# A new instruction order for a gated recurrence with a GEGLU block: weight gates out, crossbar transposes and some of the loads and stores on ScalarE's queue

## Chip, cores and metric

One core of a Trainium2 chip. The metric is the device time of one execution in microseconds (us). Each kernel was executed several times; "fast runs" are the executions that are not over 1.5% above the fastest one of the same kernel, and comparisons use these. The profile of a kernel is one of its executions; its span is some 2 us shorter than the device time. In profile lines PE is TensorE (PEld its weight loads), DVE VectorE, ACT ScalarE, POOL GpSimd and SP SyncE; a q behind a name stands for that engine's instruction queue. PSUM is the memory to which TensorE writes its results; "on-chip memory" in this text is SBUF, where the other tiles lie.

## The reference

A recurrence over 768 positions, for 4 batches of 8 heads of 48 channels, followed by a GEGLU block over 3072 tokens:

```python
mag = np.sqrt(a_re * a_re + a_im * a_im)
scale = np.minimum(mag, 0.999) / (mag + 1e-06)
a_re_n, a_im_n = (a_re * scale, a_im * scale)
for t in range(S):                       # S = 768
    new_re = ar * S_re - ai * S_im       # ar, ai: a_re_n, a_im_n at t
    new_im = ar * S_im + ai * S_re
    S_re, S_im = (new_re + kv, new_im)   # kv = outer product of k and v at t
    y[:, :, t] = np.einsum('bhd,bhde->bhe', q[:, :, t], S_re)
# x = y as (3072, 384)
g = x @ w_gate                           # 384 -> 1536
gelu = 0.5 * g * (1.0 + erf(g * inv_sqrt2))
return gelu * (x @ w_val) @ w_out        # 1536 -> 384
```

## The kernel before

The sequence is cut into 24 chunks of 128 positions. A chunk's decays are cumulated as logarithms (magnitude) and phases, `q` and `k` are multiplied by them and "rotated" into `pair` (cosine and sine parts), and attention within the chunk plus a carried state gives `x`; then come the three products of the GEGLU block. The order is no scheduler's: a text lists about 1240 words, one per step, and the kernel emits them in that order, each engine running its own in order. A word is a step, its chunk, the engine (V VectorE, A ScalarE, P GpSimd, S a crossbar transpose by DMA, B a phase shift that reads PSUM) and the buffer slot:

```python
PLAN = """
ldaim2=0 si2V=0 ldare1=0 tab.LE la1=0 r1 ldare0 la0 r0 ldaim1 si1V ldare2 sr1A la2 sr0A ad1P sr2V ldaim0 r2 ln1=0
# ... (the rest cut) ...
"""
def load(nm, c, slot):                     # q, k, v, a_re, a_im
    # ... (cut) ...
    nc.sync.dma_start(out=t, in_=src[b, :, n * L:(n + 1) * L, :].transpose([1, 0, 2]))

def load_weight(piece, after):
    # ... (cut) ...
    if after:                              # the gate: a small cast that waits for another load
        # ... (cut) ...
        nc.gpsimd.tensor_copy(out=t[:, 0, 0:1], in_=a)
    nc.gpsimd.dma_start(out=t, in_=src)

def pb(c, slot, eng):                      # phase shift of a quarter turn
    t = take("ph", ("ph", c), slot).rearrange("p s h d -> p s (h d)")
    if eng == "B":                         # from PSUM
        nc.vector.tensor_scalar(out=t[:, 0], in0=T["cumt", c], scalar1=TURN / (2.0 * PI),
                                scalar2=TURN / 4.0, op0=ALU.mult, op1=ALU.add)
    else:                                  # from on-chip memory: "ph<-ph" in the profile
        nc.vector.tensor_scalar(out=t[:, 0], in0=t[:, 1], scalar1=TURN / 4.0, scalar2=None, op0=ALU.add)

def rotate(t, i, e, cs, eng):              # kp and qp: "pair<-ke,cs" and "pair<-qe,cs"
    ENG[eng].tensor_tensor(out=t[:, :, i, :, 0:D], in0=e.unsqueeze(2).to_broadcast([128, H, 2, D]),
                           in1=cs.rearrange("p s h d -> p h s d"), op=ALU.mult)

def tps(c, hg, slot, eng):
    t = take("tps", ("tps", c, hg), slot)
    if eng == "S":                         # a crossbar transpose instead of TensorE and a copy
        src = T["pair", c][:, hg * 4:(hg + 1) * 4].rearrange("p h i s d -> p (h i s d)")
        nc.sync.dma_start_transpose(out=t, in_=src)
    else:
        copy(eng, t, T["tp", c, hg])
```

## Time and profile before

| | before |
|---|---|
| median of 3 runs | 252.74 us (252.19 to 254.98) |
| the profiled run, a further one: time, span, TensorE clock granted | 255.99 us, 254.2 us, 0.972 |
| VectorE, ScalarE, GpSimd busy | 181.3, 197.4, 117.5 us |
| crossbar transposes, all issued by SyncE | 30 of `pair`, 17 of `x` |
| ScalarE's table loads | 43 |

TensorE is the fullest engine (82% of the span; ScalarE has 78%) and works to the end, so what counts is where TensorE stands still. The prediction shows the main lines of this profile. Two stretches more, in the columns of the prediction's table of stretches:

```profile
54.00:84.00 30.00, 27.40 (x402) 24.42 (x400) 27.59 (x48) 27.68 (x39) 23.73 (x29) 1.00 1.08 189
84.00:112.00 28.00, 25.28 (x248) 19.38 (x247) 21.62 (x39) 22.52 (x36) 15.63 (x15) 0.94 0.77 155
```

And the durations of VectorE's operations by line (ns, least/median/greatest):

```profile
L350 DVE TENSOR_SCALAR ph<-ph x12: 346/352/2336, 20.5 to 219.3; 128x384 int32<-128x384 int32 x12
L368 DVE TENSOR_TENSOR pair<-ke,cs x11: 541/549/559, 24.7 to 197.1; 128x768 bf16<-128x768 bf16 x11
L274 DVE TENSOR_TENSOR z<-aim,z x12: 545/550/1018, 8.6 to 162.9; 128x384 f32<-128x384 f32 x12
```

In this profile most operations of one shape share one duration, 352 ns for the phase shift; yet three of the twelve took 1159, 1743 and 2336 ns.

### The profile page before, as it was taken

To read this page: it belongs to the slowest core of one execution; us is meant where nothing else is said; L and a number is where in the kernel's file an instruction comes from. 1 tells how busy PE (TensorE), PEld (TensorE's weight loads), DVE (VectorE), ACT (ScalarE), POOL (GpSimd) and SP (SyncE) were. 2 spreads that over 40 slices of the span, in tenths; PEclk is the share of its full clock that TensorE was granted. 3 is DMA by queue.
4 is the path that set the end of the run, shared out by engine and by line. 5 is a ranking of instruction groups with operands and counts; after the bars stand their busy time and mean duration, and the time that the engine had idled before them with its cause. 6 is when DMAs were issued, how large, how long until landed. Compare 5 with 4: busy or idle time off the path is not lost.

```text
span 254.2 us, 5703 instructions
## 1 busy us (share of the span) xinstructions
PE 207.5 (82%) x2203; PEld 162.4 (64%) x2203; DVE 181.3 (71%) x321; ACT 197.4 (78%) x298; POOL 117.5 (46%) x128
## 2 busy tenths in 40 slices
PE   0125985397999999699798986999699999998994
PEld 0002654377987777487586675787686868887782
DVE  4648998298989699499597576986786556827350
ACT  4998999288899999576989788799699868735141
POOL 3211392698995783222577536623490722150000
PEclk9999997589999999799999999999999999999999
DMA  7989999999999196999999999989976696175121
GB/s 145 242 199 203 197 211 181 172 218 211 152 188 226 22 207 137 208 173 192 221 189 172 195 219 172 196 159 192 198 143 133 118 162 167 33 158 56 49 93 62
DMA packets 166059, 41.75 MB, mean 164 GB/s; under 512 B 157841, under 2 KB 165265, under 8 KB 166033
## 3 DMA queue, kind: packets, MB, share of 16 engines
q1 hardware_dynamic: 162848, 37.86, 75.5%
q0 software_dynamic: 3184, 3.54, 8.5%
q8 instruction: 17, 0.28, 0.5%
q14 instruction: 10, 0.07, 0.1%
HBM read 30.67 MB, written 4.72 MB: 139 GB/s over the span
## 4 chain that ended last, share of the span: by engine, by line
PE 36%; DMA 19%; DVE 12%; ACT 12%; issue 9%; SPq 7%; POOL 2%; POOLq 1%; DVEq 0%; ACTq 0%
PE bank L447 18%; PE bank L469 12%; SPq L230 6%; DMA k<-in_k_dram 5%; ACT L483 4%; DMA tps<-pair 4%; DMA wg<-in_moe_w_gate_dram 4%; DMA are<-in_a_re_dram 3%; DMA xt<-x 3%; DVE h L461 2%; ACT gel L457 2%; PE bank L398 2%; PE bank L323 2%; ACT cs L354 2%; DVE ssb L401 1%
## 5 line engine op out<-in xcount | busy, mean ns | idle before, releaser
L447 PE MATMUL bank<-xt,wg 128*128 128x256 bf16 (+1 forms) x468 | 56.7, 268 | 6.8 <-DMA xt<-x 5.0
L457 ACT ACTIVATE gel<-bank 128x512 bf16<-128x512 f32 x72 | 39.8, 599 | 27.1 <-PE bank L447 20.1
L461 DVE TENSOR_TENSOR h<-bank,gel 128x512 bf16<-128x512 f32 x72 | 47.4, 684 | 16.4 <-PE bank L447 11.0
L483 ACT ACT_TABLE_LOAD x43 | 55.2, 1283 | 1.5 <-PEq L509 0.8
L447 PE MATMUL bank<-xt,wv 128*128 128x256 bf16 (+1 forms) x468 | 55.2, 264 | 0.3 <-ACT gel L457 0.2
L469 PE MATMUL bank<-wo,h 128*128 128x384 bf16 x288 | 49.6, 326 | 1.6 <-ACT e L334 1.4
L447 PEld LDWEIGHTS <-wg 128*128 128x128 bf16 x468 | 42.1, 99 | 13.5 <-issue 4.0
L447 PEld LDWEIGHTS <-wv 128*128 128x128 bf16 x468 | 41.8, 98 | 5.8 <-issue 0.6
L401 DVE TENSOR_TENSOR ssb<-bank,tri 128x512 bf16<-128x512 f32 x48 | 32.3, 683 | 16.8 <-PE bank L398 13.3
L469 PEld LDWEIGHTS <-h 128*128 128x128 bf16 x288 | 27.5, 98 | 18.8 <-issue 1.9
L368 POOL TENSOR_TENSOR pair<-ke,cs 128x768 bf16<-128x768 bf16 x13 | 21.9, 1682 | 15.3 <-PE bank L469 6.7
L291 POOL TENSOR_TENSOR are<-are,s 128x384 f32<-128x384 f32 x16 | 16.4, 1030 | 21.7 <-DVE s L280 11.6
L368 POOL TENSOR_TENSOR pair<-qe,cs 128x768 bf16<-128x768 bf16 x9 | 15.5, 1724 | 18.9 <-issue 11.0
L398 PE MATMUL bank<-tps 128*128 128x128 bf16 x192 | 18.4, 223 | 5.8 <-DMA tps<-pair 2.4
L398 PEld LDWEIGHTS <-tps 128*128 128x128 bf16 x192 | 13.5, 100 | 10.1 <-issue 2.9
L354 ACT ACTIVATE cs<-ph 128x768 bf16<-128x768 int16 x24 | 19.4, 836 | 0.6 <-DVE ph L341 0.5
L333 ACT ACTIVATE e<-bank 128x384 bf16<-128x384 f32 x24 | 11.8, 491 | 6.5 <-PE bank L323 6.4
L362 POOL TENSOR_TENSOR qe<-q,e 128x384 bf16<-128x384 f32 x13 | 12.0, 925 | 10.2 <-ACT e L334 8.1
L382 PE MATMUL bank<-ident,pair 128*128 128x128 bf16 x144 | 12.4, 244 | 4.5 <-POOL pair L368 4.0
L211 DVE COPY tps<-bank 128x1024 bf16<-128x1024 bf16 x18 | 12.0, 681 | 5.6 <-PE bank L382 5.6
L274 POOL TENSOR_TENSOR z<-aim,z 128x384 f32<-128x384 f32 x12 | 12.9, 1084 | 4.8 <-ACT z L263 4.7
L359 POOL TENSOR_TENSOR ke<-k,e 128x384 bf16<-128x384 f32 x12 | 12.1, 1006 | 5.4 <-ACT gel L457 3.7
(79 smaller groups left out, 337.0 us busy)
## 6 DMA issues: line engine op xcount, KB each, us to landing
v<-in_v_dram SPq DMA_DIRECT2D x24, 192.0 KB, 4.1
q<-in_q_dram SPq DMA_DIRECT2D x24, 192.0 KB, 3.9
k<-in_k_dram SPq DMA_DIRECT2D x24, 192.0 KB, 3.8
out_dram<-o SPq DMA_DIRECT2D x24, 192.0 KB, 2.3
aim<-in_a_im_dram SPq DMA_DIRECT2D x21, 192.0 KB, 3.8
are<-in_a_re_dram SPq DMA_DIRECT2D x21, 192.0 KB, 3.8
wo<-in_moe_w_out_dram POOLq DMA_DIRECT2D x3, 384.0 KB, 6.2
wg<-in_moe_w_gate_dram POOLq DMA_DIRECT2D x1, 768.0 KB, 9.6
```

The lines of the kernel that those rows point to most:

```text
L230: nc.sync.dma_start(out=t, in_=src[b, :, n * L:(n + 1) * L, :].transpose([1, 0, 2]))
L274: ENG[eng].tensor_tensor(out=t, in0=block("aim", c), in1=t, op=ALU.mult)
L291: ENG[eng].tensor_tensor(out=t, in0=t, in1=block("s2", c), op=ALU.add)
L354: act(out=take("cs", ("cs", c), slot).rearrange("p s h d -> p (s h d)"), in_=lo[:, :, 0], func=AF.Sin, scale=2.0 * PI / TURN)
L368: ENG[eng].tensor_tensor(out=t[:, :, i, :, 0:D], in0=e.unsqueeze(2).to_broadcast([128, H, 2, D]), in1=cs.rearrange("p s h d -> p h s d"), ...
L398: nc.tensor.matmul(ps[:, hi, :], t[:, 2 * hi + 1, :], t[:, 2 * hi, :], start=True, stop=True)
L401: nc.vector.tensor_tensor(out=take("ssb", ("ssb", c, hg), slot), in0=T["sc", c, hg], in1=tri.unsqueeze(1).to_broadcast([128, 4, 128]), op= ...
L447: nc.tensor.matmul(ps[:, a], w[:, i, fc * 128:(fc + 1) * 128], T["xt", c][:, 0:n, i, :], start=(i == 0), stop=(i == NDM - 1))
L457: act(out=take("gel", ("gel", c, f), slot), in_=T["g", c, f], func=AF.Gelu)
L461: nc.vector.tensor_tensor(out=t[:, f * FW * L:(f + 1) * FW * L], in0=T["v", c, f], in1=T["gel", c, f], op=ALU.mult)
L469: nc.tensor.matmul(ps, ht[:, fc, i, :], wo_sb[:, fc, :], start=(fc == 0), stop=(fc == NFF - 1))
L483: nc.scalar.preload_act_table_set(TABLES[word[4:]])
```

## The change

The intent: SyncE's queue, which issued everything but the weights, is full in the middle of the kernel. All crossbar transposes move to ScalarE's queue, with 20 of 116 loads and 11 of 24 stores; the gates of the weight loads go; a search found a new order for two queues. In the new order ScalarE has 34 table loads instead of 43 and fewer casts and squares; VectorE has more (17 `kp` rotations instead of 11, 30 phases read from PSUM instead of 23), GpSimd 7 `kp` instead of 13, and TensorE transposes ten more sets itself (22 of `pair` instead of 18, 13 of `x` instead of 7).

```diff
-def load(nm, c, slot):
+crossbar = nc.scalar.dma_start_transpose
+def load(nm, c, slot, eng):
+    queue = nc.scalar if eng == "A" else nc.sync
-    nc.sync.dma_start(out=t, in_=src[...])
+    queue.dma_start(out=t, in_=src[...])
-    if after:
-        # ... (cut) ...
-        nc.gpsimd.tensor_copy(out=t[:, 0, 0:1], in_=a)
-    nc.sync.dma_start(out=out[c * L:(c + 1) * L, :], in_=T["o", c])
+    (nc.scalar if eng == "A" else nc.sync).dma_start(out=out[c * L:(c + 1) * L, :], in_=T["o", c])
-    if eng == "S":                       # tps and xt
-        nc.sync.dma_start_transpose(out=t, in_=src)
+    if eng == "D":
+        crossbar(out=t, in_=src)
-ldaim2=0 si2V=0 ldare1=0 tab.LE la1=0 r1 ldare0 la0 r0 ldaim1 si1V ldare2 sr1A la2 sr0A ad1P ...
+ldare2A=0 tab.LE la2=0 r2 ldare0 sr2V ldare1 ldaim1=0 ldaim0 ldaim2 la0 sr0P r0 la1 ldare3=1 ...
 (all other lines of the order differ as well)
```

## The prediction

> **What bounds the kernel now.** I read the page from its top: the busy shares, the 40 slices, then the waits of the issuing queue, then the chain that ended last, and then a table of stretches.
>
> ```profile
> PE 207.5 (82%) x2203; PEld 162.4 (64%) x2203; DVE 181.3 (71%) x321; ACT 197.4 (78%) x298; POOL 117.5 (46%) x128
> ...
> PE   0125985397999999699798986999699999998994
> ...
> ACT  4998999288899999576989788799699868735141
> ...
> DMA  7989999999999196999999999989976696175121
> ```
>
> No engine is full over the whole span, but PE is nearly full after its first eight or nine slices, and the DMA engines are nearly full for most of the first 28. The table of stretches (columns: length, then busy us and instructions of PE, PEld, DVE, ACT and POOL, PE clock, DMA share, GB/s) shows it in stages:
>
> ```profile
> 0.00:54.00 54.00, 25.84 (x229) 17.35 (x230) 37.72 (x78) 43.04 (x69) 23.62 (x36) 0.91 0.98 196
> ...
> 112.00:140.00 28.00, 25.16 (x276) 19.55 (x275) 23.38 (x40) 25.16 (x41) 15.36 (x14) 1.00 1.03 189
> 140.00:180.00 40.00, 34.48 (x338) 26.25 (x336) 30.52 (x53) 34.25 (x48) 19.20 (x18) 1.00 0.95 191
> 180.00:225.00 45.00, 44.60 (x481) 35.91 (x482) 29.44 (x51) 34.98 (x51) 18.95 (x19) 1.00 0.69 134
> ```
>
> The first 54 us are a fill: PE idles 28 us of them while loads arrive. From 54 us on PE is busy 181.7 of 200 us, so of the whole span at most 28 + 18 = 46 us of PE idleness can be attacked, and some 11 us at the start (the wait for the first phase angles, "ACT th" 11.4 us) can hardly be. In the middle PE, ACT and DMA all stand near 0.9 together: a balanced pipeline in which a queue that comes late is felt.
>
> That queue is SyncE's. It issues everything except weights, in order. Its own waits and the issue durations of its two transposes (ns, min/median/max) say:
>
> ```profile
> SPq L436 <- DVE x L211: 10.2, 2, 7.8
> ...
> SPq L388 <- POOL pair L368: 8.5, 3, 6.2
> ```
> ```profile
> L388 SPq DMA_TRANSPOSE tps<-pair x30: 1231/1352/3165, 87.3 to 227.4; - x30
> ```
>
> A transpose holds the queue 1.35 us and, while its input is late, it holds all loads and stores behind it too. With about 0.6 us a load and 0.56 us a store (read off the SyncE timeline after 100 us) the queue issues 116 x 0.6 + 24 x 0.56 + 30 x 1.35 + 17 x 1.21 = 144 us; between 87 and 190 us its timeline is issue after issue with hardly a gap. The chain that ended last carries the same signature:
>
> ```profile
> PE 36%; DMA 19%; DVE 12%; ACT 12%; issue 9%; SPq 7%; POOL 2%; POOLq 1%; DVEq 0%; ACTq 0%
> PE bank L447 18%; PE bank L469 12%; SPq L230 6%; DMA k<-in_k_dram 5%; ACT L483 4%; DMA tps<-pair 4%; DMA wg<-in_moe_w_gate_dram 4%; DMA are<-in_a_re_dram 3%; DMA xt<-x 3%; DVE h L461 2%; ACT gel L457 2%; PE bank L398 2%; PE bank L323 2%; ACT cs L354 2%; DVE ssb L401 1%
> ```
>
> The two crossbar transposes are 7% (some 17 us) of the chain, load issue 6%, the first gate weight 4%.
>
> **What the Trainium skill says.** (1) "DMA: Bandwidth & Descriptors", section "Issuing engines are not separate DMA queues": all issuers share the same 16 DMA engines, and a second issuer only saves sequencer time. The trace agrees in part: in the first 54 us the DMA share is 0.98 at 196 GB/s, so there a second queue can't bring bandwidth; but from 87 to 190 us the sequencer itself is full, so its time is worth saving. (2) The same page, "Silent corruption: two transposing streams in flight at once": transposes from SyncE and ScalarE must not overlap, which is why all of them move together; no run here shows the corruption. (3) "Perfetto Trace Analysis", sections "DVE / Act Engine Instruction" and "DMA Instruction — HWDGE": a compute instruction waits in a queue of its own while the sequencer goes on, whereas a DMA instruction keeps the sequencer through its wait, the lock on the descriptor generator and the generation. So on ScalarE a DMA issue may hide under activations that were already queued, but a late input stops everything behind it. ScalarE issues nothing in this trace, so how much hides is open; the growth of the same transpose from 1.23 to 3.17 us agrees with waits on a shared resource. (4) "ScalarE: Activation LUTs", "What ACT_TABLE_LOAD costs": about 1283 ns a load, and the trace has exactly 1283 ns; the extra drain of 1380 ns that the page adds isn't seen (the next activation starts about 1.29 us after the load starts).
>
> **The change part by part.**
>
> *ScalarE, compute.* Counting the words of the two orders: table loads 43 to 34, -9 x 1.283 = -11.5 us; phases -9 x 0.50 = -4.5; squares -8 x 0.52 = -4.2; casts of x -4 x 0.48 = -1.9; casts of v -3 x 0.51 = -1.5; one xt copy -0.5; st +2 x 0.48 = +1.0; five new evictions of 128x1024, estimated at 1.05 us from 0.48 us for 384 and 0.84 us for 768 columns, +5.3. Sum -17.8: 197.4 becomes about 180 us.
>
> *ScalarE, issue.* New: 26 tps x 1.35 = 35 us, 11 xt x 1.21 = 13, 20 loads x 0.6 = 12, 11 stores x 0.56 = 6: 66 us. If nothing hid, ScalarE would have 246 us of work, against a span of 254 whose last 29 us hold only 9.8 us of it: ScalarE would be the bound. I assume that about half hides under queued activations, so 213 us, 16 more than now.
>
> *SyncE.* 96 x 0.6 + 13 x 0.56 = 65 us in place of 144: no longer full, and loads no longer stand behind a transpose whose input is late.
>
> *VectorE.* kp +6 x 0.55, qp +0.7, phases +9 x 0.55, x +4 x 0.55, xt +7 x 0.35, the rest about -2.5: +11 us, to 192. *GpSimd*: six of the 1.68 us kp leave, squares and casts come: -4. *TensorE*: +4 tps and +6 xt sets of transposes, 32 x 86 ns + 18 x 120 ns = +4.9 us. *DMA*: 4 of 30 and 6 of 17 crossbar transposes fewer. *Weight gates*: seven small casts of 0.2 to 0.35 us, about 2 us of GpSimd; the first waits 6.1 us for a k load. PE waits only 1.4 us for that weight, so this is worth 1 to 3 us at the fill; without it the weights compete with the loads.
>
> *By stage* (adding the mean durations, less their overlaps, in program order; estimates). Until ten of 24 outputs are done, at 144 us before: TensorE 117 to 124, VectorE 114 to 128, ScalarE 115 to 116 plus 19 of issue. The fill can therefore hardly be shorter, and VectorE would need 89% instead of 79% to keep 144 us. After it: TensorE 116 to 114, VectorE 71 to 68, ScalarE 76 to 58 plus 45 of issue; before took 110 us here, so ScalarE fits only if the issue hides in part. If the freed queue takes about half of the PE waits on transposes (5.0 + 2.7 + 2.9 + 2.4 = 13 us), most of the 4 us of "ACT gel" waiting for h, and some of the late loads, 9 to 12 us come back; the extra TensorE work costs 5 and ScalarE's issue 2. Net -3 to -5 us: 249 us.
>
> **Rivals.** *A: ScalarE becomes the bound.* For it: 180 + 66 = 246 us and the in-order stop at a late pair (pair waits of 6.2 us stood on SyncE, where they cost only loads; on ScalarE they delay gelu, and so the PSUM banks). Against it: the order was searched anew, moves 18 us off ScalarE, and drops table loads. It would make 256 to 265 us. *B: the freed queue pays in full.* Loads come as soon as buffers are free, transposes no longer queue behind loads, and PE idleness after 54 us falls from 18 to 8 us, the fill by 3: 239 to 244 us. *C: it is all hidden by the DMA engines*, whose share is 0.95 to 1.09 in three of the middle stretches; then only ten transposes fewer count, against 5 us more on TensorE: 250 to 254 us.
>
> **Range and chances.** The arithmetic alone says no change or slightly slower (A and C); that the new order was found by a search, with ScalarE relieved for the purpose, speaks for B. I give B 0.42, C and the middle 0.36, A 0.22. Predicted 249 us, range 239 to 262.
>
> **What would show it.** Right: SyncE's timeline between 87 and 190 us has gaps and its wait for x and pair is gone; ACT busy near 180 us with 34 table loads; xt and tps waits of PE below 7 us; PE busy about 212 us; the first gate matmul near 54 us as before. The share of issue that hides shows as ScalarE's gaps at transposes: half of 66 us would leave some 33 us of them. Wrong: ScalarE idle ahead of gelu with "issue" or its own queue as the cause, and PE waiting for gelu (rival A); DMA share still at 1.0 with the same GB/s and PE waiting for loads (rival C); or a fill that is shorter by over 5 us, which I don't expect since VectorE and the loads bound it.

## The result, and the profile after

| | before | after |
|---|---|---|
| median, runs of the same session | 253.84 us (252.19 to 254.98, 4 runs) | 263.36 us (262.31 to 265.38, 4 runs) |
| ratio of fast runs | 1 | 1.039 (95%: 1.029 to 1.049) |
| profiled span, granted clock | 254.2 us, 0.972 | 261.0 us, 0.961 |

A ratio is the mean time of one kernel's fast runs over the mean of the other's fast runs in the same rounds, so it is not quite the ratio of the medians quoted beside it. The changed kernel is slower by 3.9%.

The page after, the lines that answer to the prediction's first:

```profile
PE 210.4 (81%) x2253; PEld 166.7 (64%) x2253; DVE 198.3 (76%) x343; ACT 182.6 (70%) x271; POOL 119.3 (46%) x127
...
PE   0138566609999999979879999499859999999994
...
ACT  4999995728899899979688896856537367414231
...
DMA  8999999899997009499975999969975947633102
```

ScalarE fell by 14.8 us, about as foreseen (182.6 against 180), and TensorE is at 210.4 (212 foreseen). VectorE rose by 17.0 us, to 198.3; 192 was foreseen. TensorE stops in the ninth slice, and the DMA engines stand still near 90 us. The stretches:

```profile
0.00:54.00 54.00, 25.72 (x244) 17.55 (x244) 46.60 (x87) 44.73 (x67) 28.42 (x37) 0.91 1.12 203
54.00:84.00 30.00, 25.01 (x372) 23.36 (x373) 27.53 (x48) 22.83 (x31) 22.21 (x25) 0.89 1.04 176
84.00:112.00 28.00, 27.96 (x276) 21.63 (x273) 21.19 (x40) 26.52 (x36) 9.96 (x11) 1.00 0.38 66
```

From 84 to 112 us the DMA share is 0.38 and TensorE is busy 27.96 of 28 us: that hole costs nothing there. Over the whole span TensorE has 210.4 - 207.5 = 2.9 us more work and 50.6 - 46.7 = 3.9 us more idleness, together the 6.8 us by which the span is longer. (The profiled run of the kernel before was slower than its four runs in the table, so the two profiles show 7.1 of the 9.5 us between the medians.) Part of the 2.9 us is probably the lower clock, 0.961 against 0.972: between d1 and d2 below, both at 0.986, TensorE's busy time differs by 0.8 us only. That is an estimate; why the clock is lower was not tested. So neither issue time nor DMA bandwidth is visibly the limit. Where is TensorE's idleness? Its longest wait after the fill, and then VectorE's and GpSimd's timelines just before that wait ends (start, duration, engine, line, operation, count; in brackets the idle time before it and what ended it):

```profile
58.84 0.50 PE L428 MATMUL bank<-ident,x 128*128 128x128 bf16 x3 [7.61 <-DVE x L212]
```
```profile
51.35 4.11 DVE L366 TENSOR_TENSOR pair<-ke,cs 128x768 bf16<-128x768 bf16 x1 [2.39 <-POOL ke L357]
55.38 2.94 DVE L348 TENSOR_SCALAR ph<-ph 128x384 int32<-128x384 int32 x3
58.24 0.54 DVE L212 CAST x<-bank 128x384 bf16<-128x384 f32 x1
```
```profile
47.74 0.50 POOL L212 CAST vb<-v 128x384 bf16<-128x384 f32 x1 [9.84 <-DMA v<-in_v_dram]
...
50.40 0.92 POOL L357 TENSOR_TENSOR ke<-k,e 128x384 bf16<-128x384 f32 x1
51.26 0.80 POOL L245 DMA_DIRECT2D wg<-in_moe_w_gate_dram  x1
52.08 1.96 POOL L272 TENSOR_TENSOR z<-aim,z 128x384 f32<-128x384 f32 x2
53.99 0.99 POOL L289 TENSOR_TENSOR are<-are,s 128x384 f32<-128x384 f32 x1
54.94 1.20 POOL L278 TENSOR_TENSOR s<-aim 128x384 f32<-128x384 f32 x1
```

TensorE stands still for 7.61 us until VectorE has copied `x` out of PSUM. VectorE comes to that copy late: it waits 2.39 us for GpSimd's `ke`, then one rotation takes 4.11 us (0.55 is normal) and three phase shifts 2.94 us together (0.35 each is normal). While these run, GpSimd, which had waited 9.84 us for a load of `v`, works without a gap. The copy of `x`, which reads PSUM, takes its normal 0.54 us.

Yet this stop alone doesn't explain the longer time. By 112 us TensorE has been busy 78.7 us here and 78.5 us before (sums of the stretches shown), so until then it stood still as long in both, 33.3 and 33.5 us. The added idleness comes later: 149.0 - 131.7 = 17.3 us against 142.2 - 129.0 = 13.2 us. The largest wait in that part is for crossbar transposes (7.1 us, 2.4 us before). The runs e3 and a2 below each take one of these two waits away.

VectorE's held operations are not only at that place. The same lines as before, over the whole kernel:

```profile
L348 DVE TENSOR_SCALAR ph<-ph x14: 344/704/1801, 55.4 to 207.4; 128x384 int32<-128x384 int32 x14
L366 DVE TENSOR_TENSOR pair<-ke,cs x17: 542/552/4108, 20.8 to 218.4; 128x768 bf16<-128x768 bf16 x17
L272 DVE TENSOR_TENSOR z<-aim,z x13: 546/621/1989, 8.0 to 166.9; 128x384 f32<-128x384 f32 x13
```

The median phase shift has doubled. The Trainium skill, "SBUF — State Buffer", section "Who interferes with whom", has a mechanism for this: VectorE and GpSimd share a pair of ports to on-chip memory. A VectorE instruction with two inputs there contends with a GpSimd instruction that reads; one in the two-port mode (which a `tensor_scalar` can enter) contends with GpSimd too. Whichever comes first keeps the ports for its whole instruction, and the other is shut out. That gives the theory to test.

What of ScalarE's issuing? The issue durations on its queue, and the piece of its timeline where a table load, two transposes and two gelus meet:

```profile
L386 ACTq DMA_TRANSPOSE tps<-pair x26: 1246/1298/2073, 107.7 to 233.4; - x26
```
```profile
140.45 1.28 ACT L481 ACT_TABLE_LOAD   x1
141.12 1.31 ACTq L386 DMA_TRANSPOSE tps<-pair  x1
141.75 1.32 ACT L455 ACTIVATE gel<-bank 128x512 bf16<-128x512 f32 x2
142.66 1.38 ACTq L386 DMA_TRANSPOSE tps<-pair  x1
```

The transposes are issued beside table loads and activations, not between them. And SyncE is not full any more; its largest waits (total us, times, longest) are now stores waiting for outputs:

```profile
SPq L248 <- DVE o L212: 61.8, 6, 17.5
SPq L248 <- DMA q<-in_q_dram: 18.2, 1, 18.2
```

### The profile page after: what moved, and what is told of

It reads as the page before. It is cut to its first block, busy times and chain, and to the rows that moved or that the text cites.

```text
span 261.0 us, 5749 instructions
## 1 busy us (share of the span) xinstructions
PE 210.4 (81%) x2253; PEld 166.7 (64%) x2253; DVE 198.3 (76%) x343; ACT 182.6 (70%) x271; POOL 119.3 (46%) x127
## 4 chain that ended last, share of the span: by engine, by line
PE 41%; DMA 17%; DVE 17%; ACT 8%; SPq 5%; issue 4%; ACTq 2%; POOL 2%; DVEq 0%; POOLq 0%
PE bank L445 23%; PE bank L467 10%; DMA v<-in_v_dram 8%; DMA tps<-pair 6%; SPq L233 5%; DVE pair L366 3%; DVE h L459 2%; PE bank L396 2%; DVE ph L348 2%; DVE ssb L399 2%; PE bank L408 2%; DMA out_dram<-o 2%; DMA are<-in_a_re_dram 2%; PE bank L321 2%; DVE z L272 1%
## 5 line engine op out<-in xcount | busy, mean ns | idle before, releaser
L445 PE MATMUL bank<-xt,wv 128*128 128x256 bf16 (+1 forms) x468 | 57.9, 267 | 0.2
L459 DVE TENSOR_TENSOR h<-bank,gel 128x512 bf16<-128x512 f32 x72 | 48.0, 685 | 12.9 <-PE bank L445 7.8
L445 PEld LDWEIGHTS <-wg 128*128 128x128 bf16 x468 | 42.8, 99 | 5.7 <-DMA xt<-x 0.4
L289 POOL TENSOR_TENSOR are<-are,s 128x384 f32<-128x384 f32 x16 | 17.2, 1078 | 29.5 <-DVE s L278 15.9
L396 PE MATMUL bank<-tps 128*128 128x128 bf16 x192 | 19.0, 229 | 13.2 <-DMA tps<-pair 7.1
L366 POOL TENSOR_TENSOR pair<-qe,cs 128x768 bf16<-128x768 bf16 x8 | 13.4, 1669 | 24.7 <-ACT cs L352 14.5
L396 PEld LDWEIGHTS <-tps 128*128 128x128 bf16 x192 | 13.7, 102 | 16.2 <-DMA tps<-pair 7.8
L360 POOL TENSOR_TENSOR qe<-q,e 128x384 bf16<-128x384 f32 x15 | 14.9, 992 | 8.0 <-ACT e L332 6.5
L212 POOL CAST vb<-v 128x384 bf16<-128x384 f32 x20 | 11.4, 587 | 13.4 <-DMA v<-in_v_dram 13.4
L366 DVE TENSOR_TENSOR pair<-ke,cs 128x768 bf16<-128x768 bf16 x17 | 14.9, 879 | 2.5 <-POOL ke L357 2.4
L380 PE MATMUL bank<-ident,pair 128*128 128x128 bf16 x176 | 14.9, 238 | 1.5 <-DVE pair L366 1.3
L278 POOL TENSOR_TENSOR are<-are 128x384 f32<-128x384 f32 x11 | 9.9, 903 | 12.0 <-ACT z L257 11.9
```

What stands on the lines that cost most here:

```text
L289: ENG[eng].tensor_tensor(out=t, in0=t, in1=block("s2", c), op=ALU.add)
L360: ENG[eng].tensor_tensor(out=take("qe", ("qe", c), slot), in0=T["q", c], in1=T["e", c][:, 0], op=ALU.mult)
L380: nc.tensor.transpose(ps[:, 2 * hi + i, :], T["pair", c][:, hg * 4 + hi, i], ident)
L396: nc.tensor.matmul(ps[:, hi, :], t[:, 2 * hi + 1, :], t[:, 2 * hi, :], start=True, stop=True)
L445: nc.tensor.matmul(ps[:, a], w[:, i, fc * 128:(fc + 1) * 128], T["xt", c][:, 0:n, i, :], start=(i == 0), stop=(i == NDM - 1))
L459: nc.vector.tensor_tensor(out=t[:, f * FW * L:(f + 1) * FW * L], in0=T["v", c, f], in1=T["gel", c, f], op=ALU.mult)
```

## The experiments

Theory G: the loss comes from GpSimd's work standing where VectorE's is, because VectorE is held off (G1) or because GpSimd's own results come late (G2). Rivals: Q, the issuing on ScalarE (or what is issued there) costs; W, the ungated weights do; T, the extra transposes on TensorE do. All ratios are to the kernel before, in the same rounds.

### 1. The new order with other issuers (Q)

```diff
 a1: crossbar = nc.sync.dma_start_transpose;  queue = nc.sync;  stores nc.sync
 a2: crossbar = nc.sync.dma_start_transpose   (loads and stores as in the change)
 a3: queue = nc.sync                          (transposes and stores as in the change)
```

> The changed kernel with every transpose, load and store issued by SyncE again: only the order (and the missing gates) is new. Theory S (issuing on ScalarE costs the time, by holding gelu and evictions behind transposes): back to 248 to 255 us. Theory O (the order itself: ten more sets of TensorE transposes, 17 us more VectorE, weights without gates): stays at 261 us or above. Ratio to before under S 0.98 to 1.01, under O 1.03 or more.

> The changed kernel with the 37 crossbar transposes on SyncE, loads and stores split as in the change. Theory S (the transposes on ScalarE are the costly part, 37 of 68 issues and about 48 of 62 us): 250 to 256 us. Theory O: within 1% of the changed kernel, 261 to 266 us.

> The changed kernel with all loads and stores on SyncE and only the transposes on ScalarE. Theory S: 260 to 266 us, as the transposes stay. A rival L (what hurts is the split of loads and stores: a load on ScalarE goes out only when ScalarE comes to it, and a store on SyncE that waits for its input holds the loads behind it): the ScalarE half of L would give 254 to 259 us here; under the SyncE half of L it stays at 263 or gets worse, since eleven more stores join SyncE's queue.

Measured: a1 265.35 us, 1.041 (1.030 to 1.051; its profiled execution was an outlier of 546 us and isn't used); a2 263.59 us, 1.036 (1.028 to 1.045); a3 262.15 us, 1.027 (1.017 to 1.037). With everything back on SyncE the new order is as slow as with ScalarE. So the issuer isn't the cause: rival Q falls, and so does the hope that the freed queue pays: in this order it is worth nothing that these runs resolve. In a2 TensorE's wait of 7.1 us for crossbar `tps` is gone, and the kernel is no faster.

### 2. Parts of the change in the old order, and stores and weights in the new

```diff
 b1: nc.sync.dma_start_transpose -> nc.scalar.dma_start_transpose   (old order)
 c1: (nc.scalar if eng == "A" else nc.sync).dma_start -> nc.scalar.dma_start   (new order, all stores)
 c2: words ldw2, ldw3 moved behind vb3P and vb4P                     (new order)
 b2: ldw0@k0 -> ldw0, and so for the other six                       (old order, no gates)
 b3: stores nc.sync.dma_start -> nc.scalar.dma_start                 (old order)
```

> The kernel before with only the issuer of its 47 crossbar transposes changed to ScalarE, order and gates untouched. Theory S: slower by 3 to 8%, 260 to 273 us, since ScalarE gets about 60 us of issue on top of 197 us of compute. Theory O: within 1.5% of before, 250 to 256 us.

> The changed kernel with all 24 stores issued by ScalarE (13 of them stood on SyncE). In the changed kernel's trace SyncE waits 61.8 us in six stores for VectorE's copy of o, 17.5 us at the longest, and the DMA engines move 0 to 18 GB/s in two slices around 85 to 98 us meanwhile. Theory P (a store in SyncE's in-order queue keeps the loads behind it back, so the loads arrive late and TensorE starves after 112 us): 254 to 259 us, and the hole in the DMA row is gone. If P is only a side effect: within 1% of the changed kernel, 261 to 266 us.

> The changed kernel with its first two weight loads moved later in GpSimd's order, each behind the cast of a v block that it kept waiting (v took 14 us to land when both weights, 1.5 MB, were issued just before it). Theory G (the ungated weights take the DMA engines from the loads that the fill needs): 256 to 260 us, and the v load lands in 5 us. Rival: the first gate matmul then waits for its weight instead and nothing is won, 261 to 267 us.

> The kernel before without its seven weight gates and nothing else. Theory G: slower by 1 to 3%, 256 to 262 us. Rival (the gates are free, since GpSimd's own order already holds the weights back): within 1%, 251 to 256 us. The prediction's step (gates worth 1 to 3 us of gain) would give 251 to 253 us.

> The kernel before with its 24 stores issued by ScalarE; loads and all transposes stay on SyncE. If relief of SyncE's queue was worth having (13 us of store waits and 13 us of store issue leave it) and short issues hide under queued activations: 247 to 252 us. If ScalarE pays for every issue: 254 to 262 us.

Measured: b1 282.01 us (276.33 to 288.28, so scattered that no fast set could be formed; even its fastest run is 8.7% above the 254.14 us of before in that session). c1 275.0 us, 1.069 (1.062 to 1.077). c2 264.64 us, 1.025 (1.014 to 1.037). b2 256.34 us, 0.993 (0.984 to 1.003). b3 255.56 us, 0.993 (0.984 to 1.001).

Moving the transposes to ScalarE in an order not made for it costs heavily (b1), and so do more stores there in the new order (c1). Removing the gates is harmless in the old order (b2), so the gates aren't the cause by themselves; loading two weights later in the new order (c2) gives back some 1.4 points, not separable from nothing. In c2 GpSimd's wait for `v` is gone from its largest waits, and yet the rotation still takes 3.43 us, the three shifts 3.02 us, and TensorE waits 6.3 us for `x`. So rival W explains a part at best, and the late `v` is not what makes VectorE's operations long.

### 3. Fewer transposes on TensorE (T)

```diff
-tp9.1=3 tps9.1V=3  tp10.1=4 tps10.1V=4  tp11.0=6 tps11.0V=2  tp13.0=2 tps13.0V=0
+tps9.1D=3          tps10.1D=4           tps11.0D=2           tps13.0D=0
-xtp8=0 xt8V=0  xtp9=0 xt9V  xtp11=0 xt11V  xtp13=6 xt13V
+xt8D=0         xt9D         xt11D          xt13D
```

> The changed kernel with eight of its 35 TensorE transpose sets (four of pairs, four of x, blocks 8 to 13) made crossbar transposes on ScalarE instead; TensorE has 4 x 0.69 + 4 x 0.36 = 4 us less to do and VectorE 4 us. Rival W (TensorE's added work is paid one for one, since TensorE is 80% busy and full after 84 us): 258 to 261 us. Theory S (transposes on ScalarE cost more than they save): 264 us or more.

Measured: 275.12 us, 1.067 (1.061 to 1.073). Returning eight sets to the crossbar makes it worse: TensorE now waits for the transposes.

```profile
PE bank L395 <- DMA tps<-pair: 13.3, 2, 9.3
...
PE bank L444 <- DMA xt<-x: 6.7, 3, 2.6
```

Against 7.1 us for `tps` in the changed kernel. The order had its places chosen for TensorE's transposes, so this run can't say what they cost by themselves; it gives rival T no support, and section 5 leaves them in place.

### 4. Phase shifts read from PSUM instead of on-chip memory (G1, a part)

If the `ph<-ph` shifts are what is held off, giving them PSUM as input should help; they keep their work otherwise.

```diff
 e1 (new order): pb6V pb7V pb8V removed; pb6B pb7B pb8B put right behind pa6A, pa7V, pa8V
 e2 (new order): the same for all 14 shifts
 b4 (old order): the same for all 12 shifts
 e3 (new order): e1, and kp4V moved behind the copy xt0V (after x0V)
```

> The changed kernel with three of its 14 phase shifts, those of blocks 6, 7 and 8, computed on VectorE straight from PSUM behind the step that reads the same bank, where the changed kernel computes them later from SBUF to SBUF. Theory D (VectorE is held off by GpSimd's back-to-back SBUF operations: the SBUF-to-SBUF shifts of 0.35 us took 2.9 us together, and 7.8 us in the run with all loads on SyncE, and the key rotation before them 4.1 us, so that x and TensorE's transposes of x came 7 us late at 51 to 58 us): 257 to 260 us, TensorE's wait for x under 3 us. Rival W (it is the ten extra sets of TensorE transposes and the places of the steps): within 1%, 261 to 265 us.

> The changed kernel with all 14 SBUF-to-SBUF phase shifts taken from PSUM instead (each 0.55 us in place of 0.35 us undisturbed, 0.74 us as measured). Theory D: at least as good as with three, 255 to 260 us; VectorE's busy time falls by 2 to 4 us. Rival W: 261 to 266 us.

> The same edit on the kernel before (12 shifts, mean 0.70 us against 0.35 us at best, so some 4 us lost to GpSimd in all, none of it in a place where TensorE waited long). Theory D: 250 to 254 us, 0 to 1.5% faster than before. Rival: no effect or slower by up to 1%.

> e1 with one word more moved: block 4's key rotation, which took 4.1 us on VectorE at 53 us instead of 0.55 us while GpSimd ran back to back, is placed behind the copies that TensorE waits for. Theory D at this place: TensorE's wait of 4.5 us for x goes, the first 84 us hold 3 us less idle time, and the end comes 2 to 4 us earlier than e1 (ratio to before 1.015 to 1.025). If the time saved there is given back later: ratio 1.03 to 1.04 as before.

Measured: e1 265.28 us, 1.032 (1.027 to 1.036); e2 268.54 us, 1.044 (1.038 to 1.049); b4 261.31 us, 1.018 (1.013 to 1.022); e3 262.1 us, 1.027 (1.018 to 1.035). None repairs it; e1, e2 and b4 miss what theory D foretold, and e3 comes near it. In e1 the three shifts are short again, but the rotation behind them is held instead, and TensorE still waits 5.1 us for `x`:

```profile
53.23 4.06 DVE L365 TENSOR_TENSOR pair<-ke,cs 128x768 bf16<-128x768 bf16 x1
```

In e3 that rotation stands behind `x` and a copy that follows it. It is short again, and TensorE's waits for `x` fall to 1.0 us, from 8.1 us in the changed kernel:

```profile
54.03 0.96 DVE L365 TENSOR_TENSOR pair<-ke,cs 128x768 bf16<-128x768 bf16 x1
```
```profile
PE bank L427 <- DVE x L211: 1.0, 2, 0.5
```

So the long stop is gone, and still the kernel is 2.7% slower than before, against 3.9% with the stop and 3.2% in e1; the intervals of the three overlap. The stop is a part of the loss at most. In b4 and e2 the shifts also come at an earlier place in VectorE's order, before other work (they must follow `pa` while the bank still holds the phases), and that may be what costs: b4 loses 1.8%, with VectorE as busy as before (182.3 us), in an order where little was held off. So these runs neither prove nor refute G1; they show that curing one place isn't enough.

### 5. GpSimd almost idle (G against all rivals)

Each of GpSimd's elementwise operations works on its first column only, in both orders. Their outputs are wrong, which doesn't matter for the times. Memory is filled with zeros first, and the exponents are damped so that nothing overflows. All other engines keep every instruction. (In d1 to d4 the zero fills add 8.4 us to GpSimd and 2.8 us to VectorE at the start.)

```diff
+class Narrow:
+    def _n(self, x):
+        return x[(slice(None),) + tuple(slice(0, 1) for _ in x.shape[1:])]
+    def tensor_tensor(self, out, in0, in1, op):
+        nc.gpsimd.tensor_tensor(out=self._n(out), in0=self._n(in0), in1=self._n(in1), op=op)
+    # tensor_copy likewise
+ENG["P"] = Narrow()        # d1: new order, d2: old order
```

> Wrong result on purpose: the changed kernel with each elementwise GpSimd operation on the first of its columns only (and the decay exponents made near zero, so that all numbers stay finite), so that GpSimd is almost idle and cannot hold VectorE off; every instruction and wait stays. Compare with d2, the same in the old order. Theory D (the new order loses more to VectorE waiting on GpSimd, 23 us over the shortest times of the same operations in place of 13, and to GpSimd's own lateness): both become faster, this one by 8 us or more beyond the other, so that d1 over d2 is within 1.5%. Rival W (TensorE work and the places of loads and stores): d1 stays 3 to 5% above d2.

> Wrong result on purpose: the kernel before with the same edit as d1, the control. 240 to 252 us; VectorE's busy time falls by about 10 us, from the waits on GpSimd that go.

Measured: d1 (new order) 251.26 us, 0.982 (0.976 to 0.989); d2 (old order) 252.39 us, 0.990 (0.983 to 0.996). The new order's deficit of 3.9% is gone: d1 over d2 is 0.982 / 0.990 = 0.993. Both have their own queues, gates and transposes unchanged, so none of Q, W and T is needed to explain it. From the pages of d1 and of d2, and from d1 the operations that were held:

```profile
PE 205.3 (83%) x2253; PEld 162.8 (66%) x2253; DVE 178.5 (72%) x347; ACT 182.2 (73%) x271; POOL 42.1 (17%) x148
PE 204.5 (82%) x2203; PEld 160.3 (64%) x2203; DVE 171.9 (69%) x325; ACT 197.1 (79%) x298; POOL 36.6 (15%) x149
```
```profile
49.17 0.56 DVE L382 TENSOR_TENSOR pair<-ke,cs 128x768 bf16<-128x768 bf16 x1 [1.89 <-POOL ke L205]
49.65 0.92 DVE L364 TENSOR_SCALAR ph<-ph 128x384 int32<-128x384 int32 x3
50.49 0.54 DVE L228 CAST x<-bank 128x384 bf16<-128x384 f32 x1
```

The five operations that stretched from 51.35 to 58.78 us in the changed kernel, 7.4 us, take 1.9 us here, `x` is copied at 50.5 instead of 58.2 us, and the wait of 7.61 us isn't among TensorE's waits any more.

VectorE's busy time now has two parts that can be told apart. With GpSimd nearly idle the two orders differ by 178.5 - 171.9 (d2) = 6.6 us: that is VectorE's added work. With GpSimd at work they differ by 198.3 - 181.3 = 17.0 us. The other 10.4 us are stretching; the expectation for d1 has the same difference from another sum, 23 us over the shortest durations in place of 13.

### 6. GpSimd busy, but hardly reading (G1 against G2)

d1 takes away GpSimd's traffic and its lateness at once. Here GpSimd stays about as busy: its first column, then a write of constants into a buffer that nobody reads, as long as the shortest such operation took (for casts next to nothing), then its second column, for which readers wait. Results are wrong again.

```diff
 class Narrow:
     def tensor_tensor(self, out, in0, in1, op):
-        nc.gpsimd.tensor_tensor(out=self._n(out), in0=self._n(in0), in1=self._n(in1), op=op)
+        nc.gpsimd.tensor_tensor(out=self._n(out, 0), in0=self._n(in0, 0), in1=self._n(in1, 0), op=op)
+        nc.gpsimd.memset(busy[:, 0:n], 0.0)      # n by kind: 395 to 1400 columns, casts 1
+        nc.gpsimd.tensor_tensor(out=self._n(out, 1), in0=self._n(in0, 1), in1=self._n(in1, 1), op=op)
```

> Wrong on purpose, as d1: the new order, but GpSimd is kept as busy as in the changed kernel (about 105 to 120 us): each of its operations becomes its first column, then a write of constants into a buffer that nobody reads, as long as the operation's own duration (its shortest in the trace), then its second column, for which the readers wait. So GpSimd is as late as before, but it hardly reads on-chip memory while VectorE works. Theory P (VectorE's operations with two inputs in on-chip memory are held off while GpSimd reads): the two-input operations of VectorE (pair, z, are) run at about 0.55 us each again, VectorE's busy time falls from 198 to near 180 us, and the time is near d1, 0.975 to 1.00 of before. Theory L (it is GpSimd's own lateness that costs): VectorE's busy time falls too, but the time stays near the changed kernel, 1.025 to 1.045. Phase shifts from memory to memory (one input) may still stretch.

> Wrong on purpose: the same replacement in the old order, as the base for d3. Theory P: as d2, about 0.985 to 1.00 of before, and d3 over d4 within 1%. Theory L: 1.00 of before, and d3 over d4 about 1.03 to 1.04.

Measured: d3 (new order) 255.99 us (252.31 to 257.83, 6 runs), 1.001 (0.992 to 1.010); d4 (old order) 253.28 us (252.52 to 255.75), 1.000 (0.993 to 1.007). d3 over d4 is 1.001 by fast runs and 1.011 by medians of all runs; d3 scatters, and three of its six runs were slow. Its profiled execution is one of these (span 256.1 us), so from it only the busy times and durations of operations are taken:

```profile
PE 211.4 (83%) x2253; PEld 166.8 (65%) x2253; DVE 183.5 (72%) x347; ACT 182.7 (71%) x271; POOL 114.0 (45%) x368
```
```profile
L374 DVE TENSOR_SCALAR ph<-ph x14: 346/402/1542, 50.3 to 201.3; 128x384 int32<-128x384 int32 x14
L392 DVE TENSOR_TENSOR pair<-ke,cs x17: 539/546/590, 22.0 to 213.0; 128x768 bf16<-128x768 bf16 x17
L298 DVE TENSOR_TENSOR z<-aim,z x13: 537/547/559, 8.1 to 159.8; 128x384 f32<-128x384 f32 x13
```

GpSimd is busy 114.0 us, of which 8.4 are the zero fills; the other 105.6 us stand against 119.3 in the changed kernel, so it is a little less late as well. VectorE falls from 198.3 to 183.5 us, zero fills included. Operations with two inputs in on-chip memory are never held (the rotation's greatest is 590 ns instead of 4108, that of all kinds 598); the one-input phase shifts still are (up to 1542 ns, d1: 368). That is just the distinction of the skill's page: two inputs contend with a GpSimd instruction that reads, not with one that only writes, and the two-port mode contends with either. Of the deficit of 3.75% by medians of all runs (263.36 over 253.84), 1.1% is left by the same measure, or 0.1% by fast runs. So most of it, some 70% by these medians from different sessions, goes when GpSimd stops reading. That fits G1, though the 13.7 us by which GpSimd is less busy may have a share (G2); what is left is G2, the phase shifts that are still held, or scatter.

### 7. A version that beats both

b2 and b3 each came out at 0.993, not separable from 1. Together:

```diff
 old order:  ldwN@xx -> ldwN  and  nc.sync.dma_start(out=out...) -> nc.scalar.dma_start(out=out...)
```

> The two edits to the kernel before that were at 0.993 each, together: no weight gates, and its 24 stores on ScalarE. If they add: 0.985 to 0.99. If each was noise: 0.995 to 1.005.

Measured: 251.68 us, 0.986 (0.979 to 0.993), results right: the fastest correct kernel here, 1.4% under the kernel before. So two simple ideas of the change, no gates and a second queue for stores, are worth a little in the old order. VectorE is busy 187.9 us in this kernel, more than in the kernel before (181.3), and it is still faster. It runs the same 321 VectorE instructions, so these 6.6 us are stretching, which here costs nothing that can be seen: VectorE's total alone doesn't decide. Where it makes TensorE wait may decide, but that isn't shown.

## Why the prediction was wrong

It said 249 us with 239 to 262 and gave "slower" 0.22; the kernel takes 263.36. By its own steps:

- *The step that failed: "VectorE ... +11 us, to 192", and "if the freed queue takes ... 9 to 12 us come back".* The first is a sum of counts by mean durations, as if a duration belonged to the operation. VectorE rose by 17.0 us to 198.3: the added work is 6.6 us (d1 and d2), and 10.4 us come on top from operations held off while GpSimd works. With GpSimd's work shrunk in both orders the new one is no slower (0.993). By which path the held operations cost TensorE its time stays open. The stop of 7.61 us at 51 to 58 us is the one that can be seen, but e3 has it no more and is still at 1.027. The profile before had the sign, three of twelve phase shifts over 1 us against a median of 352 ns.
- *The second half of that step*: nothing came back from the freed queue. SyncE did become free (its largest waits are now stores waiting for outputs), but a1, with every issue on SyncE, is as slow as the change. TensorE's waits on transposes, foreseen to fall below 7 us, are 7.1 us for `tps` from the crossbar alone and 4.7 us for those copied by VectorE. The 13 us of such waits that it started from count the same stops twice: 5.0 and 2.4 us are the matmuls' waits, 2.7 and 2.9 us those of the weight loads just before them. TensorE stood 7.4 us.
- *ScalarE, compute*: right, 182.6 us against 180, with 34 table loads.
- *ScalarE, issue*: mis-sized. Half of 66 us was to show as gaps; a1 and a2 show no gain from taking the issue away, and the timeline shows transposes issued beside table loads and activations.
- *TensorE*: +4.9 foreseen, +2.9 measured (+0.8 from d2 to d1, at equal clocks), from a total that was right within 2 us. *GpSimd*: -4 foreseen, +1.8 measured.
- *Weight gates, 1 to 3 us*: the size agrees with b2 in the old order (0.7%, not separable from nothing). In the new order GpSimd waited 9.84 us for a load of `v` that was issued beside two ungated weights, but issuing those later (c2) removed that wait and not the held operations.
- *Rivals*: A foretold 256 to 265 us, but by ScalarE as the bound, which a1 to a3 refute: the right time for a wrong reason. B fell. C, that DMA hides it all, missed with 250 to 254 us; the share was 0.38 in a stretch in which TensorE was never busier (27.96 of 28 us).

What stays open: where after 112 us the new order loses TensorE's time; how the loss splits between held VectorE operations and GpSimd's own lateness; and why b1 scatters so much. The clock is open too. It was 0.953 to 0.961 in the changed kernel's runs, 0.976 to 0.986 in d1's fast runs and 0.965 to 0.980 in d3's. GpSimd's dummy data changes the numbers that TensorE multiplies, but in the old order that hardly moves the clock (fast runs of d2 0.978 to 0.986, of before beside it 0.972 to 0.984; of d4 0.970 to 0.979, of before beside it 0.977 to 0.980).

## What to carry to other kernels

Before moving elementwise work to VectorE, look at the least, median and greatest duration of each of its operations, not at means: here the same-shaped operations that sometimes took several times their least were held off while GpSimd worked, and the new order, which adds more of them, raised VectorE's busy time by 17.0 us where the added work was 6.6. To find out whether another engine is the cause, shrink all of its work to one column in both kernels and compare the two: that pair of runs showed here what the twelve before it had only circled. Then check that the visible wait is the costly one: taking away the longest one (e3) brought back about one point, not separable from nothing. And try the simple parts of a change alone in the old order: here two of them together (b5, 0.986) were worth more than the whole (1.039).

## What the Trainium skill lacked or had wrong

- "SBUF — State Buffer" (section "Who interferes with whom") gives the mechanism, and d3 agrees with its distinction of reading and writing (two-input operations at most 598 ns under a writing GpSimd, 4108 ns under a reading one). It lacks that a held operation can lose several times in a row: the rotation that began at 51.35 us lasted 4.11 us, while GpSimd's records show a run of separate instructions of some 1 us each. It goes the other way as well: in d1 a GpSimd operation on one column, 0.19 us as a rule, took 3.14 us from 15.8 us on while VectorE ran six two-input operations. The page also gives no way to see it in a profile: the hold is inside the busy time, not in a wait.
- "ScalarE: Activation LUTs" adds a drain of 1380 ns to a table load; here the next activation starts 1.29 us after the load begins, and crossbar transposes are issued during it.
- "DMA: Bandwidth & Descriptors" says that a second issuer only saves sequencer time. Here it saved none that mattered in one order (1.041 with SyncE alone, 1.039 with both) and cost at least 8.7% in another (b1, fastest run), and that page doesn't warn of the latter.
- No page has that a store on one queue can wait for a load of the other: SyncE stood 18.2 us at a store until a `q` load issued by ScalarE had landed, with which it shares no buffer. In the trace the store waits for the semaphore that this load raised, and raises the same one itself. It cost nothing here, since the store's output was copied only at 220.8 us, 10.4 us later.
